# Moving four weight sums, a turn, the third unit's values and two exponentials, and cutting other products into column halves, in a fused attention and gated feed-forward kernel

## The chip, the cores and the metric

The kernel runs on one core of one Trainium2 chip. The metric is the device time of one execution in microseconds, as the median of a few runs. The core has four engines that compute: PE (TensorE, matrix products; its weight loads are listed apart as PEld), DVE (VectorE), ACT (ScalarE) and POOL (GpSimd). SP only starts DMA transfers here. The engines work through their own queues in order and meet at semaphores.

## What is computed

Sliding-window causal attention (batch 8, 8 heads, 576 positions, head size 64, window 64) is followed by a gated feed-forward layer on the 4608 resulting tokens (512 features, 1536 hidden):

```python
scores = scale * np.matmul(q, k.transpose(0, 1, 3, 2))
rel = pos[:, None] - pos[None, :]
mask = (rel >= 0) & (rel < 64)
scores = np.where(mask, scores, -1000000000.0)
attn = np.exp(scores - scores.max(-1)) ; attn = attn / (attn.sum(-1) + 1e-09)
x = np.matmul(attn, v)            # to (4608, 512)
gate = np.maximum(x @ w_gate, 0.0)
val = x @ w_val
out = (gate * val) @ w_out
```

## The kernel before

**Tiles.** The 4608 tokens are cut into tiles t=0 to t=9 of 384, 192, 448 and then 512 columns (`widths`). Attention works in windows of 64 positions; the first tokens come from units u of 192 positions (u=0, 1, 2), the rest from quads qd of four windows, two quads to a tile. For each tile the order is: scores (`q_st`, L277: 128 tiny instructions, a weight load and a matmul for each of 64 blocks), exponentials on ACT (`q_exp`, L450), masks on DVE (`q_mask`, L459), values (`t_pv`, L493: 64 weight loads and 64 matmuls of 65 columns for each half of the heads), reciprocals and scaling on DVE (L507, L515), a turn into the layout of the next product (L521), and sums of blocks of x (`x_form`, L537). Units do the same with `u_st`, `u_exp`, `u_mask`, `u_pv` (L348), `u_recip` and so on, called through `plan_exps` and `plan_values`.

**Feed-forward.** Tiles 0 and 1 use plain products: `first_hidden` and `hidden` (L634) multiply blocks of w_gate and w_val with x, ACT applies the relu (L605) and DVE multiplies the two (the gate, L609, L613, L614), and `output` (`out_mm`, L1135) multiplies by w_out. A product in `SPLIT` runs as two column halves; `halves` says how many blocks of one weight start as a group whose first two steps of four run for all, before the last two, so that the second half of the weight may land later. `OUT_SPLIT` says from which f on `out_mm` cuts its 512 columns in two, up to the last but one. From t=2 on, `fast_hidden` forms the two hidden products of each pair of blocks by seven products, P1 to P7, in place of eight (L740), which needs sums of weight blocks (`w_form`, L561, into `us` for w_gate and `vs` for w_val) and of x blocks. For a block j, the product P1 is copied by ACT to a second bank (a seed, L749), P6 and P7 are added in the first bank and copied out in between (snaps, L759); DVE adds (L776), ACT applies relu (L782, L809), DVE or POOL multiply (L765). From t=4 on, the output product is also formed with seven products (`SevenOut`, L956). `HALVED` names the products of `fast_hidden` that run as two column halves: each of its four matmuls becomes two with 128 columns, each with its own weight load.

**Order.** All is written out by hand through `Weaver`: `W.at(T, fn)` puts work into a heap at a planned time, `W.clock` is advanced by the planned length of PE's products, and `W.advance` issues what is due. The planned times only set the order in which instructions are put into the engines' queues; what an engine waits for at run time is settled by semaphores. `one_bank`, `two_banks` and `bank` hand out the eight PSUM banks; `W.pop` issues planned work until a bank is free.

**What the change touches.** `scores` (exponentials of a quad at planned times), the constants `SPLIT`, `OUT_SPLIT` and `HALVED`, the plan of the third unit's values (`plan_values(27.0, 2)`), the plan of turning q and k of batch 2 (`plan_batch(2, ...)`, executed at L200 on DVE), the list of weight sums by time, and the call of `hidden(0, ...)` with its groups. POOL copies v's rows for the third unit (`v_spread`, L216), and issues most loads (L160 weights, L162 w_out, L180 q and k, L206 v).

Of the kernel before, what the change touches and what calls it, by code (L numbers as in the profile page):

```python
# [47 lines left out]
def kernel(  # L48
# [10 lines left out]
    nc = tc.nc  # L59
# [8 lines left out]
    NF = DF // 128  # L68
    G = 4
    scale = 1.0 / float(D) ** 0.5  # L70
    TT = 2 * U
# [70 lines left out]
    W = Weaver()  # L142
# [33 lines left out]
    def qk_load(b, name, hh):  # L176

        tile_ = nat[b, name, hh] = nats[:, 2 * "kq".index(name) + hh]
        src = (q if name == "q" else k)[b, G * hh:G * hh + G]
        nc.gpsimd.dma_start(tile_, src.rearrange("h (i j) d -> (h i) (j d)", i=32))  # L180
# [241 lines left out]
    def read(to, give):  # L422
        unread.discard(id(to))
        if give:
            free.append(to)
# [4 lines left out]
    def q_wins(qd):  # L430
        return range(NQ // 64 - QW if qd == 1 else QW)

    def q_st(qd, banks=None):

        d = quads[qd] = {"st": banks or [bank() for _ in range(G)], "p": [None] * G}
        unread.update(map(id, d["st"]))
        run_rows([[st_block(d["st"][g][:, 256 * hh + 64 * i:256 * hh + 64 * i + 64], g, hh, q_window(qd, i), False, hh + i > 0)
                   for hh in range(2) for i in q_wins(qd)] for g in range(G)])
        written.update((id(to), 512) for to in d["st"])
        return 0.72  # L440

    def q_part(qd, p):
        return p.rearrange("p (h i) c -> p h i c", h=2)[:, :, 0:len(q_wins(qd))]

    def q_exp(qd, g, give=True):
        d = quads[qd]
        d["p"][g] = a_p.tile([128, 2 * QW, 64], FP16, name="pw", tag="p")
        n = 64 * len(q_wins(qd))
        if n == 256:
            nc.scalar.activation(d["p"][g].rearrange("p n c -> p (n c)"), d["st"][g], ACT.Exp, scale=scale)  # L450
        else:
            nc.scalar.activation(q_part(qd, d["p"][g]), d["st"][g].rearrange("p (h n) -> p h n", h=2)[:, :, 0:n]
                                 .rearrange("p h (i c) -> p h i c", c=64), ACT.Exp, scale=scale)
        read(d["st"][g], give)
# [10 lines left out]
    def scores(qd, T, banks=None, give=True):  # L465

        W.clock += q_st(qd, banks)
        for g in range(G):
            late = 0.8 if qd > 8 and qd % 2 and g == G - 1 else 0.0
            W.at(T + 0.8 + 0.6 * g + late, lambda g=g: q_exp(qd, g, give))  # L470
            W.at(T + 1.5 + 0.6 * g + late, lambda g=g: q_mask(qd, g))

    def t_pv(t, hh, banks, give):
# [89 lines left out]
    def plan_batch(b, load, trans):  # L563
        for i, (name, hh) in enumerate((n, hh) for n in "kq" for hh in range(2)):
            if load is not None:
                W.at(load if isinstance(load, float) else load[i], lambda name=name, hh=hh: qk_load(b, name, hh))
            if trans is None:
                continue
            W.at(trans[i], lambda name=name, hh=hh: qk_trans(b, name, hh))
# [7 lines left out]
    def plan_values(T, u):  # L577
        W.at(T, lambda: u_pv(u))
        W.at(T + 0.6, lambda: u_recip(u))
        for hh in range(2):  # L580
            W.at(T + 0.8 + 0.5 * hh, lambda hh=hh: u_norm(u, hh))
        W.at(T + 1.8, lambda: u_turn(u))
# [7 lines left out]
    def hidden(t, spans, f0=0, f1=NF, each=1, halves={}, split=(), banks=None):  # L590

        if t == 1:
            gs[2] = g_sb_p.tile([128, NF, WT], FP16, name="g_sb"), {}
        g_sb, done = gs[0]
        xt = xt_tile(t)
        n = spans[0][1] - spans[0][0]

        w = 512 // n
        each = max(each, w)

        def part(tile):
            return tile[:, 0:w * n].rearrange("p (w n) -> p w n", w=w)

        def relu(r_sb, h1):
            nc.scalar.activation(part(r_sb), part(h1), ACT.Relu)  # L605

        def gate(f, c0, r_sb, h2):
            if t == 0:
                nc.vector.tensor_tensor(g_sb[:, f:f + w, c0:c0 + n], part(r_sb), part(h2), MUL)  # L609
                done.update(dict.fromkeys(range(f, f + w), c0 + n))  # L610
                return
            m = WT - TT
            nc.vector.tensor_tensor(g_sb[:, f:f + w, TT:WT], part(r_sb)[:, :, 0:m], part(h2)[:, :, 0:m], MUL)  # L613
            nc.vector.tensor_tensor(gs[2][0][:, f:f + w, 0:n - m], part(r_sb)[:, :, m:n], part(h2)[:, :, m:n], MUL)  # L614
            done.update(dict.fromkeys(range(f, f + w), WT))
            gs[2][1].update(dict.fromkeys(((b, -1) for b in range(f, f + w)), True))

        for fb in range(f0, f1, each):
            r2s = [f_sb.tile([128, 2, WT], FP32, name="pr", bufs=4) for _ in range(2)]
            r_sbs = {}  # L620
            for i, wt in enumerate((wg, wv)):
                items = [(c0, f) for c0, _ in spans for f in range(fb, fb + each, w)]
                first = halves.get((fb, i), 1)
                for group in [items[:first]] + [[item] for item in items[first:]]:
                    hs = [singles[banks.pop(0)] if banks else one_bank() for _ in group]
                    part_written(hs)
                    for cs in ((0, 1), (2, 3)) if len(group) > 1 else (range(NC),):
                        for (c0, f), h in zip(group, hs):
                            for b in range(w):
                                W.advance(W.clock)  # L630
                                w_need(wt, f + b, cs[-1] // 2)
                                m = n // 2 if (i, f) in split else n
                                for c, lo in ((c, lo) for c in cs for lo in range(0, n, m)):
                                    nc.tensor.matmul(h[:, b * n + lo:b * n + lo + m], wt[:, c, (f + b) * 128:(f + b) * 128 + 128],  # L634
                                                     xt[:, c, c0 + lo:c0 + lo + m], start=(c == 0 and lo == 0 and not (len(group) > 1 and b)),
                                                     stop=(c == NC - 1), skip_group_check=len(group) > 1 or m < n)
                                W.clock += len(cs) * (n + 7) / 2400.0
                            if cs[-1] < NC - 1:
                                continue
                            if i == 0:  # L640
                                r_sb = r_sbs[c0, f] = r2s[len(r_sbs) // 2][:, len(r_sbs) % 2]
                                W.at(W.clock, lambda r_sb=r_sb, h=h: relu(r_sb, h))
                            else:
                                W.at(W.clock, lambda f=f, c0=c0, r_sb=r_sbs[c0, f], h=h: gate(f, c0, r_sb, h))
# [55 lines left out]
    def fast_hidden(t, seven=None):  # L700
# [23 lines left out]
        def product(j, name, i):  # L724
# [10 lines left out]
            w, x = operands(name, *kinds[i], j)  # L735
            step = HT // 2 if (t, j, name) in HALVED else HT
            for m in range(2):
# [434 lines left out]

    LAST = len(widths) - 1
    BY_ACT = ()
    SPLIT, OUT_SPLIT = [(0, 4 + i) for i in range(8)] + [(1, 4 + i) for i in range(4)], 3
    HALVED = ((4, 0, 'P5'),)
    FAST_OUT = (LAST - 5, LAST - 4, LAST - 3, LAST - 2, LAST - 1, LAST)
    O_FORMS = {3: [(1.4, 2, 0), (1.5, 2, 1), (1.6, 2, 2), (1.7, 0, 0), (1.8, 0, 1), (6.5, 0, 2), (9.0, 1, 0), (14.2, 1, 1), (14.3, 1, 2)],
               4: [(4.3 + 0.1 * j, 3, j) for j in range(3)]}
# [8 lines left out]
    with tc.manual_schedule():  # L1188
# [63 lines left out]
        w_load(*V3[2], 29.6)  # L1252
        W.at(22.0, lambda: u_st(2))
        plan_exps(22.0, 2)
        plan_values(27.0, 2)

        v_spread(2, pool)
        for name in "kq":
# [18 lines left out]
        W.at(36.4, lambda: v_spread(3, pool))  # L1277
        for u in (4, 5):
            W.at(41.9, lambda u=u: v_spread(u, dve))
        plan_batch(2, (36.5, 36.6, 38.0, 38.1), (52.9, 53.0, 57.5, 62.0))  # L1280
        W.at(50.5, lambda: behind_x(2))
        for u in (6, 7):
            W.at(38.2, lambda u=u: v_load(u))
# [46 lines left out]
                    qk_loads(t + 3, ends - QAT)  # L1330

        sums = {w: [(w, j, n) for j in range(NF // 4) for n in (0, 1, 3, 2)] for w in (0, 1)}
        for T, gap, eng, some in ((16.2, 0.0, nc.vector, sums[0][:4]), (20.9, 0.0, nc.vector, sums[1][:4] + sums[0][4:8]),
                                  (29.7, 0.0, nc.vector, sums[1][4:6]),
                                  (44.7, 0.1, nc.gpsimd, sums[1][6:8] + sums[0][8:10]), (50.6, 0.1, nc.gpsimd, sums[0][10:12] + sums[1][8:])):
            for i, (w, j, n) in enumerate(some):
                W.at(T + gap * i, lambda eng=eng, w=w, j=j, n=n: w_form(eng, (wg, wv)[w], n, j))
# [10 lines left out]

        W.advance(15.3)
        first_hidden()  # L1350
        hidden(0, ((0, TT),), 4, NF, 4, split=SPLIT, halves={(8, 0): 3, (8, 1): 2})
        hidden(1, ((0, U),), each=4, banks=[0, 1, 4, 5, 2, 3, 0, 1, 2, 3, 0, 1])
        taken["one"] += 2
        output(0, (0, 1, 2, 3), (0, 4, 8, NF))
# [4 lines left out]
        for t in range(2, LAST + 1):  # L1359
# [30 lines left out]
            qd = 2 * (t + 1 - NS)  # L1390
# [39 lines left out]
```

## Time and profile before

| | us |
|---|---|
| median of 3 runs (lowest to highest) | 301.84 (301.57 to 301.95) |
| the profiled execution: its own time | 301.29 |
| its span, first to last instruction | 299.6 |
| PE busy in the span | 288.8 |
| DVE busy | 256.7 |
| ACT busy | 198.7 |
| POOL busy | 193.9 |

Where the time goes by stage, with PE's busy time in it (from the view of stretches of time):

| stretch | what runs | length | PE busy |
|---|---|---|---|
| 20.0 to 38.5 | hidden products of t=0 and t=1, third unit | 18.5 | 18.08 |
| 38.5 to 53.8 | first scores of t=2, output of t=0 and t=1 | 15.3 | 15.18 |
| 53.8 to 116.3 | t=2 and t=3 | 62.5 | 62.44 |
| 116.3 to 147.8 | t=4 | 31.5 | 30.90 |
| 147.8 to 178.1 | t=5 | 30.3 | 30.30 |
| 178.1 to 209.2 | t=6 | 31.1 | 30.52 |
| 209.2 to 239.5 | t=7 | 30.3 | 30.30 |
| 239.5 to 299.6 | t=8, t=9 and the end | 60.1 | 56.55 |

How to read the lines that follow. A line of the timeline has the start, the time from the first start to the last end of the merged instructions, the engine, the line of the kernel, the operation, output and inputs, the tile shape and, with an x, how many; in brackets the idle time of that engine just before and what ended it. Matmuls are pipelined: one lasts some 0.2 us longer than its distance to the next, so lengths of runs are taken from start to start. A line of the view of stretches has the stretch, its length, and for each engine the busy time and the number of instructions begun. "Issue" is time in which an engine waited for nothing that the profile shows.

### The profile page before, as it was taken

The page shows a single profiled execution, that of the slowest core. Times are in us where ns is not written, and L with a number is a line of the kernel's source. Part 1 is how long each engine was busy: PE and PEld are TensorE (multiplying, and loading weights), DVE is VectorE, ACT ScalarE, POOL GpSimd, SP SyncE. Part 2 cuts the span into 40 slices and gives each one's busy share as a digit, 9 for nine tenths or more (in the row PEclk, how much of TensorE's full clock was granted, in tenths as well). Part 3 has the DMA queues.
Part 4 walks back from the last instruction along what each step waited for, and adds up shares of the span by engine and source line. Part 5 has one row for each costly group of instructions (what it writes and reads, how often), then busy time and mean ns, then how long its engine had stood idle before and what let it go on. Part 6 is the DMA issues. An engine that isn't in the chain of part 4 may idle for free.

```text
span 299.6 us, 10994 instructions
## 1 busy us (share of the span) xinstructions
PE 288.8 (96%) x4627; PEld 242.2 (81%) x4627; DVE 256.7 (86%) x513; ACT 198.7 (66%) x400; POOL 193.9 (65%) x223
## 2 busy tenths in 40 slices
PE   4899999999999999999999999999999999999995
PEld 2488878996588756888888888878888888888894
DVE  5989987797889799899999999989858986896585
ACT  3744361888378848974898479846985698637850
POOL 8767668897369926785948595859276607441751
PEclk9999999999999999999999999999999999999999
DMA  7999999966946489901599239924910210021013
GB/s 216 181 197 195 193 194 200 221 68 120 161 128 113 82 150 173 116 18 39 80 210 105 66 61 216 116 64 55 179 30 19 83 47 0 3 83 61 1 38 105
DMA packets 59122, 32.86 MB, mean 110 GB/s; under 512 B 39488, under 2 KB 53440, under 8 KB 59072
## 3 DMA queue, kind: packets, MB, share of 16 engines
q0 software_dynamic: 46688, 18.29, 52.5%
q1 hardware_dynamic: 11808, 13.41, 15.1%
q8 instruction: 36, 0.59, 0.8%
q10 hardware_dynamic: 576, 0.46, 0.5%
q14 instruction: 14, 0.11, 0.1%
HBM read 37.75 MB, written 9.44 MB: 158 GB/s over the span
## 4 chain that ended last, share of the span: by engine, by line
PE 89%; DVE 6%; DMA 1%; issue 1%; ACT 1%; DVEq 0%
PE bank L740 48%; PE bank L956 19%; PE bank L874 5%; PE bank L634 4%; PE bank L1135 4%; PE bank L493 3%; PE bank L277 3%; DVE kT L200 2%; PE bank L672 1%; DMA vs<-in_k_dram 1%; DVE qT L200 1%; DVE pw L459 1%; PE bank L348 1%; DVE p L318 1%; ACT pw L450 1%
## 5 line engine op out<-in xcount | busy, mean ns | idle before, releaser
L765 POOL TENSOR_TENSOR g_sb<-pr 128x512 f16<-128x512 f32 (+1 forms) x36 | 45.2, 1256 | 41.8 <-ACT pr L782 41.5
L776 DVE TENSOR_TENSOR pr<-bank,pr 128x512 f32<-128x512 f32 (+1 forms) x96 | 60.9, 674 | 3.3 <-PE bank L740 1.9
L759 ACT COPY pr<-bank 128x512 f32<-128x512 f32 (+1 forms) x96 | 51.0, 587 | 14.0 <-PE bank L740 13.9
L765 DVE TENSOR_TENSOR g_sb<-r,bank 128x512 f16<-128x512 f32 (+1 forms) x48 | 32.5, 677 | 22.7 <-ACT r L809 21.0
L956 PEld LDWEIGHTS <-g_sb 128*128 128x128 f16 x444 | 41.8, 98 | 5.1
L740 PE MATMUL bank<-xc,vs 128*128 128x256 f16 (+2 forms) x292 | 42.7, 269 | 0.3 <-ACT pw L450 0.3
L740 PE MATMUL bank<-xc,us 128*128 128x256 f16 (+2 forms) x292 | 42.7, 269 | 0.0
L740 PEld LDWEIGHTS <-vs 128*128 128x128 f16 x388 | 37.6, 98 | 4.3 <-issue 0.5
L740 PEld LDWEIGHTS <-us 128*128 128x128 f16 x388 | 37.6, 98 | 3.8
L206 POOL DMA_DIRECT2D v<-in_v_dram x41 | 34.7, 866 | 9.1 <-PE bank L740 3.2
L782 ACT ACTIVATE pr<-pr 128x512 f32<-128x512 f32 (+1 forms) x48 | 30.2, 630 | 8.4 <-DVE pr L776 8.4
L450 ACT ACTIVATE pw<-bank 128x512 f16<-128x512 f32 x60 | 32.1, 606 | 2.1 <-PE bank L277 1.7
L809 ACT ACTIVATE r<-bank 128x512 f32<-128x512 f32 (+1 forms) x48 | 28.7, 598 | 5.4 <-PE bank L740 4.7
L740 PEld LDWEIGHTS <-wg 128*128 128x128 f16 x288 | 28.0, 98 | 3.2
L740 PEld LDWEIGHTS <-wv 128*128 128x128 f16 x288 | 28.1, 98 | 2.9
L740 PE MATMUL bank<-xt,wg 128*128 128x256 f16 (+1 forms) x192 | 28.5, 271 | 0.0
L740 PE MATMUL bank<-xt,wv 128*128 128x256 f16 (+1 forms) x192 | 28.5, 271 | 0.0
L906 POOL TENSOR_TENSOR g_sb<-g_sb,xus 128x512 f16<-128x512 f16 x24 | 27.0, 1144 | 0.0
L956 PE MATMUL bank<-wo,g_sb 128*128 128x256 f16 (+1 forms) x222 | 26.6, 270 | 0.0
L749 ACT COPY bank<-bank 128x512 f32<-128x512 f32 (+1 forms) x48 | 25.6, 573 | 0.0
L956 PE MATMUL bank<-wts,g_sb 128*128 128x256 f16 (+1 forms) x222 | 25.6, 270 | 0.0
L459 DVE TENSOR_TENSOR pw<-pw,mask 128x512 f16<-128x512 f16 x60 | 23.5, 437 | 2.1 <-ACT pw L450 1.7
(125 smaller groups left out, 521.1 us busy)
## 6 DMA issues: line engine op xcount, KB each, us to landing
out_dram<-o_sb SPq DMA_DIRECT2D x31, 256.0 KB, 3.7
nats<-in_k_dram POOLq DMA_DIRECT2D x15, 288.0 KB, 5.9
nats<-in_q_dram POOLq DMA_DIRECT2D x15, 288.0 KB, 7.0
v<-in_v_dram POOLq DMA_DIRECT2D x31, 128.0 KB, 7.7
v<-v SPq DMA_DIRECT2D x12, 132.0 KB, 2.4
v<-v SPq DMA_DIRECT2D x24, 66.0 KB, 2.0
wg<-in_moe_w_gate_dram POOLq DMA_DIRECT2D x6, 256.0 KB, 6.7
wv<-in_moe_w_val_dram POOLq DMA_DIRECT2D x6, 256.0 KB, 8.5
```

What stands on the lines that cost most here:

```text
L206: nc.gpsimd.dma_start(v16s[b % 2][lo:hi, g, :, 0:64], v[b, :, 64 * g - 64 + lo:64 * g - 64 + hi].rearrange("h p d -> p h d"))
L450: nc.scalar.activation(d["p"][g].rearrange("p n c -> p (n c)"), d["st"][g], ACT.Exp, scale=scale)
L459: nc.vector.tensor_tensor(d["p"][g], d["p"][g], mask[:, None, :].to_broadcast([128, 2 * QW, 64]), MUL)
L740: nc.tensor.matmul(to[:, HT * m + lo:HT * m + lo + step], w[:, k, 128 * m:128 * m + 128], x[:, k, lo:lo + step], start=(first and m == 0 a ...
L749: nc.scalar.copy(at[j, "B", i][:, 0:TW], at[j, "A", i][:, 0:TW])
L759: nc.scalar.copy(pr[:, i], at[j, "A", i][:, 0:TW])
L765: eng.tensor_tensor(gh[:, f:f + 2, h], pair(r), pair(v), MUL)
L776: nc.vector.tensor_tensor(pr[:, i], to[:, 0:TW], pr[:, i], ADD)
L782: nc.scalar.activation(pr[:, 0], pr[:, 0], ACT.Relu)
L809: nc.scalar.activation(r, to[:, 0:TW], ACT.Relu)
L906: eng.tensor_tensor(to, x, y, op)
L956: nc.tensor.matmul(at[key][:, QN * m * whole:QN * m * whole + n1 - n0], A[:, 128 * m:128 * m + 128], B[:, c, n0:n1] if len(B.shape) == 3 e ...
```

## The change

The exponentials of quad 7 get other planned times (the third and fourth later, the second earlier). `SPLIT` now has all eight blocks f=4 to 11 of both weights, where it had all eight of w_gate and four of w_val. `OUT_SPLIT` goes from 3 to 7. `HALVED` takes in P1, P2, P3 and P4 of block j=1 in t=4, beside P5 of j=0. The third unit's values are planned at 26.4 in place of 27.0, the last turn of q of batch 2 at 60.0 in place of 62.0. The four sums of w_gate's second block (`sums[0][4:8]`) move from 20.9 to 45.55, still on DVE. The groups of the last four blocks in `hidden(0, ...)` become 4 and 3, from 3 and 2.

```diff
         for g in range(G):
             late = 0.8 if qd > 8 and qd % 2 and g == G - 1 else 0.0
-            W.at(T + 0.8 + 0.6 * g + late, lambda g=g: q_exp(qd, g, give))
+            W.at(T + 0.8 + ((0.0, 0.3, 1.6, 1.9)[g] if qd == 7 else 0.6 * g + late), lambda g=g: q_exp(qd, g, give))
             W.at(T + 1.5 + 0.6 * g + late, lambda g=g: q_mask(qd, g))
...
-    SPLIT, OUT_SPLIT = [(0, 4 + i) for i in range(8)] + [(1, 4 + i) for i in range(4)], 3
-    HALVED = ((4, 0, 'P5'),)
+    SPLIT, OUT_SPLIT = [(i, f) for i in range(2) for f in range(4, NF)], 7
+    HALVED = [(4, 0, 'P5')] + [(4, 1, name) for name in ('P1', 'P2', 'P3', 'P4')]
...
         plan_exps(22.0, 2)
-        plan_values(27.0, 2)
+        plan_values(26.4, 2)
...
-        plan_batch(2, (36.5, 36.6, 38.0, 38.1), (52.9, 53.0, 57.5, 62.0))
+        plan_batch(2, (36.5, 36.6, 38.0, 38.1), (52.9, 53.0, 57.5, 60.0))
...
-        for T, gap, eng, some in ((16.2, 0.0, nc.vector, sums[0][:4]), (20.9, 0.0, nc.vector, sums[1][:4] + sums[0][4:8]),
+        for T, gap, eng, some in ((16.2, 0.0, nc.vector, sums[0][:4]), (20.9, 0.0, nc.vector, sums[1][:4]), (45.55, 0.0, nc.vector, sums[0][4:8]),
                                   (29.7, 0.0, nc.vector, sums[1][4:6]),
...
-        hidden(0, ((0, TT),), 4, NF, 4, split=SPLIT, halves={(8, 0): 3, (8, 1): 2})
+        hidden(0, ((0, TT),), 4, NF, 4, split=SPLIT, halves={(8, 0): 4, (8, 1): 3})
```

In the built programs PE has 9311 instructions in its list where it had 9247, 64 more; DVE, ACT, POOL and SP have as many as before. On PE the third unit's values (L348) now stand ahead of the last group of w_gate. On DVE the four sums stand ahead of the reciprocals of t=2's first values, and the turn of q one gate and one sum earlier. On ACT one exponential of quad 7 stands ahead of a seed copy (L749). POOL's and SP's orders are the same.

## The prediction

> **What bounds the kernel now.** I read the page first (busy shares, queues, chain), then the list of PE's waits, then PE's timeline around each wait, then the instruction counts at those moments.
>
> ```profile
> PE 288.8 (96%) x4627; PEld 242.2 (81%) x4627; DVE 256.7 (86%) x513; ACT 198.7 (66%) x400; POOL 193.9 (65%) x223
> ...
> q8 instruction: 36, 0.59, 0.8%
> ```
>
> PE sets the end: it is busy for 96% of the span and has 89% of the chain that ended last. The granted clock is 9 tenths or more in every slice, so time can only come out of PE's idle stretches. The queue "instruction" is the program itself being read: 36 packets in 0.59 MB, 16 KB each. PE runs 4627 weight loads and 4627 matmuls: 9254 / 36 = 257, so a packet holds about 256 PE instructions.
>
> ```profile
> PE bank L956 <- issue: 0.6, 1, 0.6
> PE bank L634 <- DVE g_sb L609: 0.4, 1, 0.4
> PE bank L740 <- ACT pw L450: 0.3, 1, 0.3
> PE bank L493 <- issue: 0.3, 1, 0.3
> ```
>
> These are all of PE's waits of 0.3 us and more after the first 15.2 us. Two are on engines, two on "issue", which is nothing the profile names. The list counts idle time after the modelled end of a matmul, so I take the lost time from starts.
>
> ```profile
> 137.90 1.32 PE L493 MATMUL bank<-v,pw 128*32 128x65 f16 x127
> 139.48 0.19 PE L493 MATMUL bank<-v,pw 128*32 128x65 f16 x1 [0.26 <-issue]
> 139.60 1.48 PE L956 MATMUL bank<-wts,xus 128*128 128x256 f16 x12
> ...
> 168.66 1.34 PE L493 MATMUL bank<-v,pw 128*32 128x65 f16 x128
> 169.93 1.48 PE L956 MATMUL bank<-wts,xus 128*128 128x256 f16 x12
> ...
> 200.27 0.94 PE L956 MATMUL bank<-wts,xus 128*128 128x256 f16 x7
> 201.78 0.71 PE L956 MATMUL bank<-wts,xus 128*128 128x256 f16 x5 [0.58 <-issue]
> ```
>
> The same 128 value products (t_pv for both halves) take 137.90 to 139.60 = 1.70 us in t=4 and 168.66 to 169.93 = 1.27 us in t=5: 0.43 lost. In t=6 the stop comes seven matmuls later; the chain has 200.34 to 204.67 = 4.33 us for 32 matmuls where t=5 has 170.00 to 173.60 = 3.60: 0.73 lost. In t=7 the same piece is 231.31 to 234.99 = 3.68: 0.08 lost.
>
> ```profile
> 0.00:139.20 139.20, 132.78 (x2270) 104.74 (x2271) 121.52 (x241) 88.42 (x190) 100.62 (x126) 1.00 0.97 147
> 0.00:201.50 201.50, 194.53 (x3294) 159.00 (x3295) 180.37 (x355) 133.64 (x276) 144.50 (x174) 1.00 0.90 137
> 0.00:232.40 232.40, 225.15 (x3806) 185.96 (x3807) 205.09 (x404) 156.25 (x319) 164.24 (x194) 1.00 0.85 128
> ```
>
> This is the key view: PE matmuls and weight loads begun before each stop (first two counts). Sums: 4541 = 17 x 256 + 189, 6589 = 25 x 256 + 189, 7613 = 29 x 256 + 189. All three stops stand on one boundary modulo 256, so PE has run out of fetched program. The instruction packets fit: narrow windows of the DMA view put one at 136.9 and one at 199.2, each some 1.4 us long, and PE resumes 2.6 us after each begins (139.48, 201.78); the next begin 1.16 us after PE resumes (140.6, 202.9). (A packet's length is its busy share in such a window, times 16 engines.) So a block is usable about 3.7 us after PE enters the one ahead of it (1.16 + 2.6; less by what is read ahead). A burst of 256 value instructions eats a whole block in 1.1 us. It stalls where a boundary lies at the start of that burst: 4285, 6333 and 7357 are PE's counts within 25 instructions of the bursts' starts (4286 at 137.85).
>
> **The change, part by part.** Instruction counts and order are those of the two built programs.
>
> *1. Four products in halves (HALVED), and what it does to every later boundary.* P1 to P4 of j=1, t=4, for both weights: 32 matmuls of 256 columns become 64 of 128. The already halved P5 has eight from 118.15 to 118.60, 56 ns each; L740's 152 in 16.59 us are 109 each. 64 x 0.0557 - 32 x 0.109 = +0.08 us. But PE's later instructions all stand 64 further on (L493 of t=4 moves from 4279 to 4343 in the order). The boundaries fall 32 matmuls, or 32 x 0.109 = 3.5 us, earlier before each burst, and the next one inside the burst, some 192 to 216 instructions in, about 0.9 us after its start. Time from entering to needing: 3.5 + 0.9 = 4.4 us and read-ahead on top, against 3.7: the three stops go, -0.43 - 0.73 - 0.08 = -1.24 us. Next late candidate: the block entered inside the burst. In t=4 it must last through the rest of the burst (0.28), 32 matmuls with both mode changes (3.6 + 0.1) and 128 score instructions (0.6): 4.6 us against 3.7. It holds by 0.9; in t=5 to 7 by 0.5 to 1.3 more, as the boundary drifts 8 instructions a tile. t=8 splits its values in two bursts 28 matmuls apart; none fills a block. Bounds: 0 (all stops reappear elsewhere) to -1.24.
>
> A page of the Trainium skill speaks against halving: "TensorE: Matmul & The Clock Gate", Back-to-back issue gap, gives some 81 ns for each 128-column matmul in a stream with its weight loads. By it the 64 would cost 64 x 0.081 - 32 x 0.109 = +1.7 us and the sum would be near 302; this trace has 56 ns for exactly such pairs and disagrees.
>
> *2. More of w_val's in halves (SPLIT), fewer of w_out's (OUT_SPLIT).* 16 matmuls of 384 columns (29.88 to 32.48: 162.5 ns) become 32 of 192 (17.56 to 20.20: 82.5): +0.04. In the output 16 of 512 (216 ns, L874) replace 32 of 256: -0.03. The two move the boundary by +32 and back to 0 before t=2, so t=2 and t=3 see the old boundaries.
>
> *3. Four sums of w_gate moved from 20.9 to 45.55, the third unit's values from 27.0 to 26.4, groups of 4 and 3 (halves).*
>
> ```profile
> 24.41 1.85 POOL L216 COPY v<-v 64x512 f16<-64x512 f16 x2 [3.30 <-DMA v<-in_v_dram]
> 26.07 0.49 PE L634 MATMUL bank<-xt,wg 128*128 128x192 f16 x4
> 26.98 0.49 PE L634 MATMUL bank<-xt,wg 128*128 128x192 f16 x4 [0.42 <-DVE g_sb L609]
> ```
>
> DVE loses 22.47 to 24.05 = 1.58 us there, so masks and gates come early and PE's stop of 0.58 (26.98 less 26.07 less 4 x 0.0825) goes. What ends last next: the values now stand ahead of w_gate's last group and need POOL's copies, which end at 26.26: PE, ready at 26.16, starts at about 26.33. It keeps 0.4 us as far as 38.5. There the scores need DVE's gates and the turn of q:
>
> ```profile
> 36.75 1.23 DVE L200 STREAM_TRANSPOSE qT<-nats 128x576 f32<-128x576 f32 x1
> ...
> 38.16 0.27 DVE L614 TENSOR_TENSOR g_sb<-pr,bank 128x128 f16<-128x128 f32 x1
> ```
>
> DVE runs without a gap from 31.13 to 38.43, PE's scores start at 38.51: DVE is already just in time. Its run starts on w_val's f=8, which the grouping of 3 now finishes at 29.45 + 16 x 0.0825 = 30.77 against 29.88 + 6 x 0.1625 = 30.86. So of 0.4 us only 0.1 passes 38.5. A stop of about 0.28 at 52.3 (boundary 1726 = 6 x 256 + 190, its packet at 50.5 amid a full DMA) probably eats half of that: -0.05 us, bounds -0.5 (all passes) to +0.2 (that packet comes as late and DVE slips). The sums at 45.55 lie in DVE's idle 1.54 us before L507 at 47.27; 1.58 overruns by 0.05, and the t=2 products that need this chain (xc, 53.53 against P6 at 55.33) have 1.8 us of cover.
>
> *4. A turn of q from 62.0 to 60.0.* It steps ahead of one gate and one sum at 64.16 to 65.74 on DVE; the bank of that gate is next needed at 67.98, the relu behind that sum starts at 66.79 and the sum would end near 66.3. Nothing; without that cover at most its own 1.25 us.
>
> *5. Two exponentials of qd 7.* On ACT only one pair changes places: the exponential of bank 2 goes ahead of the first seed copy L749.
>
> ```profile
> 117.02 0.57 ACT L749 COPY bank<-bank 128x512 f32<-128x512 f32 x1
> ...
> 117.50 0.60 ACT L450 ACTIVATE pw<-bank 128x512 f16<-128x512 f32 x1
> ...
> 118.15 0.61 PE L740 MATMUL bank<-xc,vs 128*128 128x128 f16 x8 [0.35 <-ACT pw L450]
> ```
>
> PE is ready at 117.20 + 8 x 0.056 = 117.64 and starts at 118.15: 0.51 lost. The exponential can now start at 116.43 + 0.48 = 116.91 and end at 117.51: no wait. ACT then stays full until 119.46 (the second exponential pair ends the queue ahead of the P6 snaps), so PE's P7, due 0.5 earlier at 119.83, waits for the snap's end near 119.99, and its second half again 0.05: 0.2 is given back. -0.3, bounds -0.5 to 0.
>
> **Sum.** -1.24 + 0.08 + 0.01 - 0.05 + 0 - 0.30 = -1.50 us. The profiled execution is 301.29 (span 299.6 and 1.7 around it), so 299.8 for it; the median of the runs shown is 301.84, 0.55 above, so 300.3.
>
> **The rivals.**
> A. *The early gain passes too*: DVE's transposes slip with PE and the stop at 52.3 goes: a further -0.4 to -0.7, 299.8. For: 1.58 us do leave DVE. Against: its gapless run to 38.43.
> B. *The stops only change place*: a boundary at some other burst costs what the old cost. Then -0.05 - 0.30 + 0.09 remains, 301.6. For: t=4's margin is 0.9 us, and the packet for 1726 needed 5.6 us (47.0 to 52.7) in a full DMA. Against: DMA moves little from 135 to 142 (share 0.1).
> By the Trainium skill ("Runtime: NRT & Kernel Launch", Instruction fetch mechanics) a block is 256 instructions, which the counts above confirm, and crossing one is mostly hidden, which would also give this rival's time; the three stops at +189 disagree.
> C. *Halved products wait for their weights*: PEld's own row is 98 ns a load. If loads did not overlap, 64 x 0.098 - 32 x 0.109 = +2.8 us instead of +0.08, 303.0. It decides from 79 ns a matmul (64 x 0.023 = 1.5 us); against it stands the 56 ns of P5.
>
> **Chances.** Forecast 0.62, A 0.15, B 0.15, C and the like 0.08. About 0.2% (0.6 us) is what a measurement can tell from no change. The forecast's own range is 299.7 to 301.0; with A and B the range is 299.5 to 301.6. Faster by over 0.2% (under 301.2): forecast and A, 0.77. Within: B and a little of C, 0.16. Slower: 0.07.
>
> **What would show it.** No "issue" wait of PE at L493 and L956; the tile from 178.1 to 209.2 falls from 31.1 to the 30.3 of its neighbours; counts at any stop left again at 189 modulo 256, now elsewhere. Values of u=2 start near 26.3 and scores at 38.4. P5's second half starts right after the first, and P7 shows a small ACT wait. New L740 rows of 128 columns at 56 ns. Wrong if PE stops appear at score bursts near 143, or if PE's stops vanish and the span stays.

## The result, and the profile after

| | before | after |
|---|---|---|
| median of 6 runs each (lowest to highest) | 301.89 (301.57 to 302.45) | 299.44 (299.15 to 299.69) |
| the profiled execution: its own time | 301.29 | 299.69 |
| its span | 299.6 | 298.0 |

The ratio is 0.9916, 95% interval 0.9903 to 0.9929: the change makes the kernel 2.45 us faster by the medians. The forecast was 1.50 faster (300.3). The sign held; the size fell short by 0.95 us, below the forecast's own range (299.7 to 301.0) and just under the 299.5 of the range with rivals A and B.

From the page of the changed kernel, PE's share and the packets of program:

```profile
PE 287.5 (96%) x4659; PEld 241.8 (81%) x4659; DVE 256.0 (86%) x513; ACT 198.5 (67%) x400; POOL 194.0 (65%) x223
...
q8 instruction: 36, 0.59, 0.8%
```

PE does 32 matmuls more and is as full as before; the program is read in as many packets. All of PE's waits in the changed kernel (engine, tile and line, what it waited for, total, times, longest):

```profile
PE bank L244 <- DVE bias L130: 4.4, 1, 4.4
PE bank L277 <- DVE qT L200: 0.8, 2, 0.5
PE bank L672 <- DVE xt L391: 0.7, 1, 0.7
PE bank L672 <- DMA wv<-in_moe_w_val_dram: 0.4, 1, 0.4
PE bank L241 <- ACT p L311: 0.2, 1, 0.2
PE bank L348 <- ACT p L311: 0.2, 1, 0.2
```

The two "issue" waits at L493 and L956 are gone, and so are those of L634 on DVE and of L740 on ACT. One is new: L672 waits for a load of w_val near 17.5. From start to start that is 0.52 us lost. It is nearly this execution's alone: of the other profiles only that of e6_nohalved has it, with 0.11 (see also the second profiles below).

The chain of waits of the changed kernel around t=6's values (start, length, what):

```profile
198.27 1.27 PE bank L493 x119
199.54 3.60 PE bank L956 x32
```

The 32 output matmuls after the values take 3.60, as in the undisturbed t=5 of before, where t=6 took 4.33. In t=4 the 128 values start at 137.53 and L956 at 138.81: 1.28, where it was 1.70. Stretches of the changed kernel (stretch, length, busy time and instructions of PE, PEld, DVE, ACT and POOL, then granted clock, DMA share, GB/s):

```profile
147.00:177.30 30.30, 30.30 (x510) 26.75 (x509) 28.76 (x56) 22.58 (x45) 21.93 (x25) 1.00 0.75 114
177.30:207.60 30.30, 30.30 (x511) 26.74 (x509) 28.76 (x56) 22.58 (x44) 21.89 (x23) 1.00 0.73 113
207.60:237.90 30.30, 30.30 (x511) 26.69 (x509) 24.74 (x52) 22.66 (x45) 17.55 (x18) 1.00 0.52 79
```

Tiles 5, 6 and 7 now take 30.3 us each with PE busy throughout; t=6 took 31.1.

The early part, PE's timeline of the changed kernel around the third unit's values and its first scores of t=2 (two windows):

```profile
23.84 2.80 PE L634 MATMUL bank<-xt,wv 128*128 128x192 f16 x32
26.58 0.56 PE L348 MATMUL bank<-v,p 128*32 128x65 f16 x48
27.07 0.42 PE L634 MATMUL bank<-xt,wg 128*128 128x192 f16 x3
...
37.64 0.82 PE L634 MATMUL bank<-xt,wg 128*128 128x192 f16 x8
38.39 0.95 PE L277 MATMUL bank<-qT,kT 32*128 32x64 f16 x64
```

The values follow the products with no stop (23.84 + 32 x 0.0825 = 26.48, and the 0.1 that this change of shape takes in every profile). Inside the 64 scores lies a stop of 0.27: the first starts at 38.39 and the next at 38.67. DVE's timeline shows what is late, a gate that ends at 38.61:

```profile
36.95 1.22 DVE L200 STREAM_TRANSPOSE qT<-nats 128x576 f32<-128x576 f32 x1
38.02 0.40 DVE L613 TENSOR_TENSOR g_sb<-pr,bank 128x256 f16<-128x256 f32 x1
38.35 0.26 DVE L614 TENSOR_TENSOR g_sb<-pr,bank 128x128 f16<-128x128 f32 x1
```

At the start of t=4 (PE's timeline) P5's second half follows the first, and P7 waits a little:

```profile
117.01 0.61 PE L740 MATMUL bank<-xc,us 128*128 128x128 f16 x8
117.46 0.61 PE L740 MATMUL bank<-xc,vs 128*128 128x128 f16 x8
...
119.23 0.60 PE L740 MATMUL bank<-xt,wv 128*128 128x256 f16 x4
119.84 0.60 PE L740 MATMUL bank<-xc,us 128*128 128x256 f16 x4
120.33 0.60 PE L740 MATMUL bank<-xc,vs 128*128 128x256 f16 x4
120.77 0.61 PE L740 MATMUL bank<-xt,wg 128*128 128x128 f16 x8
121.21 0.61 PE L740 MATMUL bank<-xt,wv 128*128 128x128 f16 x8
```

119.23 to 119.84 is 0.61 where four take 0.44: 0.17 lost, and 0.05 more before 120.33. The new matmuls of 128 columns come eight in 0.445 us, 56 ns each.

### The profile page after: what moved, and what is told of

Read it like the earlier page. It is cut to its first block, busy times and chain, and to the rows that moved or that the text cites. A ratio compares the mean times of both kernels' runs of the same rounds, so it can differ in the third digit from the quotient of the medians.

```text
span 298.0 us, 11057 instructions
## 1 busy us (share of the span) xinstructions
PE 287.5 (96%) x4659; PEld 241.8 (81%) x4659; DVE 256.0 (86%) x513; ACT 198.5 (67%) x400; POOL 194.0 (65%) x223
## 4 chain that ended last, share of the span: by engine, by line
PE 90%; DMA 3%; POOL 3%; DVE 2%; issue 1%; ACT 0%; DVEq 0%; POOLq 0%
PE bank L740 49%; PE bank L956 19%; PE bank L634 6%; PE bank L874 5%; PE bank L1135 4%; PE bank L277 3%; PE bank L493 3%; DMA wv<-in_moe_w_val_dram 3%; POOL v L206 1%; PE bank L672 1%; DVE kT L200 1%; DVE pw L459 1%; POOL wg L160 0%; POOL nats L180 0%; POOL wv L160 0%
## 5 line engine op out<-in xcount | busy, mean ns | idle before, releaser
L956 PEld LDWEIGHTS <-g_sb 128*128 128x128 f16 x444 | 41.8, 98 | 5.0
L740 PE MATMUL bank<-xc,us 128*128 128x256 f16 (+2 forms) x292 | 42.7, 269 | 0.0
L740 PE MATMUL bank<-xc,vs 128*128 128x256 f16 (+2 forms) x292 | 42.7, 269 | 0.0
L740 PEld LDWEIGHTS <-vs 128*128 128x128 f16 x392 | 37.7, 98 | 3.9
L740 PEld LDWEIGHTS <-us 128*128 128x128 f16 x392 | 37.7, 98 | 3.9 <-issue 0.2
L206 POOL DMA_DIRECT2D v<-in_v_dram x41 | 34.7, 866 | 6.4 <-DMA wo<-in_moe_w_out_dram 2.5
L782 ACT ACTIVATE pr<-pr 128x512 f32<-128x512 f32 (+1 forms) x48 | 30.3, 631 | 8.4 <-DVE pr L776 8.4
L740 PEld LDWEIGHTS <-wg 128*128 128x128 f16 x300 | 28.4, 98 | 3.1
L740 PEld LDWEIGHTS <-wv 128*128 128x128 f16 x300 | 28.4, 98 | 2.7
L740 PE MATMUL bank<-xt,wg 128*128 128x256 f16 (+2 forms) x200 | 28.5, 267 | 0.0
L740 PE MATMUL bank<-xt,wv 128*128 128x256 f16 (+2 forms) x200 | 28.5, 267 | 0.0
L956 PE MATMUL bank<-wo,g_sb 128*128 128x256 f16 (+1 forms) x222 | 26.6, 270 | 0.0
L749 ACT COPY bank<-bank 128x512 f32<-128x512 f32 (+1 forms) x48 | 25.6, 577 | 0.0
L956 PE MATMUL bank<-wts,g_sb 128*128 128x256 f16 (+1 forms) x222 | 25.6, 270 | 0.0
```

The source lines that it names most:

```text
L206: nc.gpsimd.dma_start(v16s[b % 2][lo:hi, g, :, 0:64], v[b, :, 64 * g - 64 + lo:64 * g - 64 + hi].rearrange("h p d -> p h d"))
L740: nc.tensor.matmul(to[:, HT * m + lo:HT * m + lo + step], w[:, k, 128 * m:128 * m + 128], x[:, k, lo:lo + step], start=(first and m == 0 a ...
L749: nc.scalar.copy(at[j, "B", i][:, 0:TW], at[j, "A", i][:, 0:TW])
L782: nc.scalar.activation(pr[:, 0], pr[:, 0], ACT.Relu)
L956: nc.tensor.matmul(at[key][:, QN * m * whole:QN * m * whole + n1 - n0], A[:, 128 * m:128 * m + 128], B[:, c, n0:n1] if len(B.shape) == 3 e ...
```

## The experiments

Every time below is beside runs of the kernel before on the same chip; an effect in us is the ratio less one times 301.9. A "stop" is a distance between the starts of two matmuls, less what the same pair takes elsewhere.

**One part alone.** Four kernels, each the kernel before with one part of the change.

```diff
 e1_halved
-    HALVED = ((4, 0, 'P5'),)
+    HALVED = [(4, 0, 'P5')] + [(4, 1, name) for name in ('P1', 'P2', 'P3', 'P4')]
 e2_early
-        plan_values(27.0, 2)
+        plan_values(26.4, 2)
-        for T, gap, eng, some in (..., (20.9, 0.0, nc.vector, sums[1][:4] + sums[0][4:8]),
+        for T, gap, eng, some in (..., (20.9, 0.0, nc.vector, sums[1][:4]), (45.55, 0.0, nc.vector, sums[0][4:8]),
-        hidden(0, ((0, TT),), 4, NF, 4, split=SPLIT, halves={(8, 0): 3, (8, 1): 2})
+        hidden(0, ((0, TT),), 4, NF, 4, split=SPLIT, halves={(8, 0): 4, (8, 1): 3})
 e3_exps
-            W.at(T + 0.8 + 0.6 * g + late, lambda g=g: q_exp(qd, g, give))
+            W.at(T + 0.8 + ((0.0, 0.3, 1.6, 1.9)[g] if qd == 7 else 0.6 * g + late), lambda g=g: q_exp(qd, g, give))
 e4_split
-    SPLIT, OUT_SPLIT = [(0, 4 + i) for i in range(8)] + [(1, 4 + i) for i in range(4)], 3
+    SPLIT, OUT_SPLIT = [(i, f) for i in range(2) for f in range(4, NF)], 7
```

> The kernel before with only the four products of t=4 in halves. Theory 1 (the prediction's terms hold as the one profiled execution of the kernel before gives them): the stops at L493 and L956 of t=4, t=6 and t=7 go, -1.24 + 0.08 = -1.16 us, ratio 0.996; the stops at 26.3 (0.58), 52.3 (0.28) and 117.6 (0.51) stay. Theory 2 (the instruction stops vary from execution to execution and are larger on average than in the one profiled): -1.5 to -2.0 us, ratio 0.993 to 0.995, with the same profile. Rival B (stops only change place): within 0.3 us of before, with stops at other bursts.

> The kernel before with only the early part: four sums at 45.55, third unit's values at 26.4, groups of 4 and 3. Theory 1: the stop of 0.58 at 26.3 goes, some 0.25 comes back as a wait of the scores near 38.4 for DVE, so -0.3 us; and -0.6 if the stop at 52.3 goes with it. Theory 2: -0.3 us at most, the stops of t=4, 6 and 7 as before. The prediction's own term was -0.05 us.

> The kernel before with only the exponentials of quad 7 moved. Both theories: the wait of 0.51 at 117.6 goes, about 0.25 comes back as waits of P7 for the snaps of P6, so -0.26 us, ratio 0.999; the fetch stops as before.

> The kernel before with only the two lists of split products changed. By own cost +0.04 - 0.03: no change (within 0.1 us). If the fetch boundaries between 30 and 53 us, which this shifts by 32 and back, are what ends the stop at 52.3, that stop goes: -0.28 us. All other stops as before.

| kernel | median (before 301.91) | ratio, 95% interval | effect us | forecast |
|---|---|---|---|---|
| e1_halved | 300.90 | 0.9965, 0.9952 to 0.9977 | -1.06 (-1.45 to -0.69) | -1.16 |
| e2_early | 301.19 | 0.9979, 0.9966 to 0.9992 | -0.63 (-1.03 to -0.24) | -0.05 |
| e3_exps | 301.94 | 1.0007, 0.9990 to 1.0024 | +0.21 (-0.30 to +0.72) | -0.30 |
| e4_split | 301.35 | 0.9988, 0.9976 to 1.0000 | -0.36 (-0.72 to 0.00) | +0.01 |

The halved products alone end all stops in t=4, t=6 and t=7 and gain what was worked out. The early part gains more than its forecast, and the column splits of w_val and w_out, forecast at nothing, probably gain too; the profile of e4_split shows how: the stop at 52.3 is not there. The profile of e2_early has none near 26, 0.29 inside the scores and 0.18 of the stop at 52.3. The exponentials by themselves can't be told from nothing. The profile of e3_exps has their stop of 0.51 at 117.6 gone and 0.25 of new ones before P7, as forecast; the rest of that run's time is in other stops, which are larger in it (the fetch stops of t=4, t=6 and t=7 are 0.70, 0.81 and 0.32, 1.83 in sum, against 1.24 in the profile shown of before).

**Is it the count modulo 256?** The change with 12 more halved products, so that later instructions stand 256 further on than in before rather than 64, and the change without the new halved products.

```diff
 e5_256
-    HALVED = [(4, 0, 'P5')] + [(4, 1, name) for name in ('P1', 'P2', 'P3', 'P4')]
+    HALVED = [(4, 0, 'P5')] + [(4, j, name) for j in (1, 2) for name in ('P1', 'P2', 'P3', 'P4', 'P5', 'P6', 'P7')] + [(4, 0, 'P4'), (4, 0, 'P3')]
 e6_nohalved
-    HALVED = [(4, 0, 'P5')] + [(4, 1, name) for name in ('P1', 'P2', 'P3', 'P4')]
+    HALVED = ((4, 0, 'P5'),)
```

> The changed kernel with sixteen products of t=4 in halves beside the old one, in place of four, so that PE's later instructions stand 256 further on than before, one whole fetched block: the boundaries lie again where they lay. Theory 1 (the stops depend on PE's count modulo 256): the stops of t=4, t=6 and t=7 come back at 188 or 189 modulo 256, 0.6 to 1.8 us in all, and twelve more halved products cost 0.23: 300.3 to 301.4 us, ratio 0.995 to 0.998. Rival (the halves help in another way, by finer matmuls or by delaying PE): no stops, 299.7 us, ratio 0.9925.

> The changed kernel without the four halved products. Theory 1: the three stops come back at 188 or 189 modulo 256, +1.1 us on the changed kernel, 300.5 us, ratio 0.996; the stop at 52.3 stays away and so does the one at 26.3. Theory 2 (early part and halves overlap in what they win): under +0.6 us.

e5_256 ran in 301.97 (before 302.54), ratio 0.9997, 0.9974 to 1.0020; e6_nohalved in 301.06, ratio 0.9961, 0.9948 to 0.9973. The stops are back in both. In e6_nohalved they are 0.08 in t=4, 0.64 in t=6 and 0.33 in t=7, and there is one of 0.14 in t=5; against its expectation there is also a stop of 0.24 near 26. PE's timeline of e5_256 in t=4 and t=6 (two windows):

```profile
138.46 1.32 PE L493 MATMUL bank<-v,pw 128*32 128x65 f16 x127
140.01 0.19 PE L493 MATMUL bank<-v,pw 128*32 128x65 f16 x1 [0.23 <-issue]
...
200.80 0.94 PE L956 MATMUL bank<-wts,xus 128*128 128x256 f16 x7
202.31 0.71 PE L956 MATMUL bank<-wts,xus 128*128 128x256 f16 x5 [0.58 <-issue]
```

and the instructions begun up to these two stops and that of t=7, from its stretches:

```profile
0.00:139.80 139.80, 133.62 (x2398) 106.42 (x2399) 121.59 (x241) 88.14 (x190) 100.46 (x126) 1.00 0.97 146
0.00:201.80 201.80, 195.35 (x3422) 160.67 (x3423) 180.12 (x353) 133.37 (x276) 144.35 (x174) 1.00 0.90 136
0.00:233.00 233.00, 226.04 (x3934) 187.66 (x3935) 205.14 (x405) 155.97 (x319) 164.09 (x194) 1.00 0.85 128
```

Matmuls and weight loads sum to 4797, 6845 and 7869: each 256 more than in before (4541, 6589, 7613), again 189 modulo 256. So it is the place of the boundary in the burst, not the halving itself, that ends the stops. They sum to 1.20 us here (0.40, 0.74, 0.06); the 12 products cost 12 / 4 x 0.08 = 0.24, and this execution started its products about 1.2 us later than that of the changed kernel, which lost 0.52 soon after: 1.20 + 0.24 + 0.68 = 2.12, and the spans differ by 300.1 - 298.0 = 2.1. The time of e5_256 came out above what was expected (ratio 0.995 to 0.998), with an interval that reaches into it; why that execution started later is not shown. Taken out of the whole change, the halving is worth (0.9961 - 0.9916) x 301.9 = 1.4 us.

**What of the early part?** The change with the four sums back at 20.9:

```diff
-        for T, gap, eng, some in (..., (20.9, 0.0, nc.vector, sums[1][:4]), (45.55, 0.0, nc.vector, sums[0][4:8]),
+        for T, gap, eng, some in (..., (20.9, 0.0, nc.vector, sums[1][:4] + sums[0][4:8]),
```

> The changed kernel with the four weight sums back at 20.9 on DVE, all else as changed. Theory 1 (the early part wins by taking 1.6 us off DVE ahead of the masks, which POOL's copy stretches): PE stops again for masks or gates near 26, 0.9 to 1.1 us, of which some 0.25 comes off the wait at 38.4: +0.5 to +0.9 us on the changed kernel, 300.0 to 300.3, ratio 0.9935 to 0.995. Rival (the order of the values and the groups alone does it): as the changed kernel, 299.4.

It ran in 300.05, ratio 0.9923, 0.9911 to 0.9936. The time is one that theory 1 named, but by the ratio it can't be told from the change (0.9916). PE's stops near 26 sum to 0.33, not 0.9 to 1.1, and the wait of 0.27 inside the scores is still there. So the sums matter less than I took them to: standing the values ahead of w_gate's last group fills most of the stop by itself, since PE has 48 value matmuls to do while DVE's gates come.

**The exponential pair later.** The change with the fourth exponential of quad 7 put 0.5 later, behind the snaps that P7 waits for:

```diff
-            W.at(T + 0.8 + ((0.0, 0.3, 1.6, 1.9)[g] if qd == 7 else 0.6 * g + late), lambda g=g: q_exp(qd, g, give))
+            W.at(T + 0.8 + ((0.0, 0.3, 1.6, 2.4)[g] if qd == 7 else 0.6 * g + late), lambda g=g: q_exp(qd, g, give))
```

> The changed kernel with the last exponential of quad 7 planned at 2.4 in place of 1.9, which puts it behind the first P6 snap on ACT. Theory: the wait of P7 for that snap (0.18 in t=4) goes, the second half's wait of 0.05 stays: -0.15 us, not to be told from no change by the median, but seen in the trace. If ACT's queue were not what holds P7, the wait stays.

It ran in 299.46, ratio 0.9912, 0.9898 to 0.9927: no better than the change. P7's first wait of 0.18 is gone, and the one before its second half grows from 0.05 to 0.23. ACT is full there (busy from 117.0 to 120.5 without a gap); the order only chooses which half waits.

**Both kernels profiled once more**, unedited, one run each.

> The kernel before once more, for a second profile of it. Theory (the one profiled execution of before had an unusually short early stop): the masks of the third unit take 0.7 us and more while POOL copies v, PE's stops between 25.5 and 27 sum to 0.9 to 1.1 us (profile shown before: 0.58) and the third unit's scores start after 38.8 (38.52). The rival (the profile shown is typical): 0.5 to 0.65 us and scores at 38.5. Both: the stops at 188 or 189 modulo 256 in t=4 and t=6 are there again.

> The changed kernel once more, for a second profile of it. Theory (the wait of 0.5 us for a load of w_val near 17.5 belongs to the one execution profiled): no such wait, first values of the third unit at 26.0 to 26.4, span 297.4 to 297.8. Rival (the change brings that wait, since w_val's halves now begin earlier): the wait is there again and the span stays at 298.0. Both: no stop at t=4, t=6 and t=7.

The first expectation failed. The second profile of before (its own time 300.80) has the same masks of 0.35, 0.35, 0.77 and 0.72 us, an early stop of 0.57 and scores at 38.42; its fetch stops are 0.31, 0.42 and none. The profile shown of before was not a rare one in its early part. For the changed kernel (299.77) the load of w_val is not waited for; but the execution starts its products 0.6 us later (14.41 against 13.79), a delay that is there by 9.7, so the third unit's values start at 26.68 and its span is 298.1 all the same. Neither profile of the changed kernel has a stop at t=4, t=6 or t=7. With the accidents taken out the two pairs give 299.6 - 298.0 + 0.5 = 2.1 us and 299.1 - 298.1 + 0.6 = 1.6.

What the second profile of the changed kernel adds is POOL and DVE around v's copy (two timelines, cut into windows so that each instruction has its line):

```profile
23.72 0.60 POOL L216 COPY v<-v 64x512 f16<-64x512 f16 x1 [2.85 <-DMA v<-in_v_dram]
24.38 1.05 POOL L216 COPY v<-v 64x1024 f16<-64x1024 f16 x1
...
23.92 0.62 DVE L318 TENSOR_TENSOR p<-p,mask 128x384 f16<-128x384 f16 x1 [0.85 <-ACT p L311]
24.46 1.19 DVE L318 TENSOR_TENSOR p<-p,mask 128x384 f16<-128x384 f16 x1
...
26.31 0.35 DVE L318 TENSOR_TENSOR p<-p,mask 128x384 f16<-128x384 f16 x1
```

The same mask takes 0.35 us by itself and 0.62 or 1.19 beside a copy. The copies end at 24.32 and 25.43, the masks at 24.54 and 25.65: both 0.22 later, as if a mask could only begin its work when the copy was over. In e3_exps it is 24.53 and 25.65 against 24.74 and 25.85. A gate (L609), which has one input in a PSUM bank, takes 0.54 us with a copy beside it or without.

**Is it POOL's copy?** Before, and the change, with that copy made by a DMA:

```diff
 e11_copy_dma (before), e12_after_dma (the change)
-        v_spread(2, pool)
+        v_spread(2)
```

> Before, with the copy of v's rows for the third unit made by a DMA in place of POOL; nothing else. Theory (POOL's copy stretches DVE's masks and sums): all masks of the third unit take 0.34 to 0.36 us, PE's stop near 26 falls under 0.3 us, and the time falls by 0.2 to 0.6 us if the DMA lands before the values need it (about 26.5), else the values wait for it. Rival (the masks vary by themselves or by DMA traffic): some masks still take 0.7 us or more and the stop stays at 0.6 to 1.1.

> The changed kernel with that copy made by a DMA; nothing else. Theory: masks at 0.35 us; the values of the third unit stand earlier here (26.1 to 26.6), so the DMA must land by 26.2; if it does, the time is 299.2 to 299.5 (the gain is lost at 38.4, where DVE's gates set the start of the scores), if it lands later it is 299.5 to 300.5. Rival (DVE's stretch still costs in the changed kernel): 298.8 to 299.1.

DVE's timeline of e11_copy_dma:

```profile
23.94 0.89 DVE L318 TENSOR_TENSOR p<-p,mask 128x384 f16<-128x384 f16 x3
24.75 0.55 DVE L609 TENSOR_TENSOR g_sb<-pr,bank 128x384 f16<-128x384 f32 x1
25.21 0.35 DVE L318 TENSOR_TENSOR p<-p,mask 128x384 f16<-128x384 f16 x1
```

All four masks take 0.35 us and PE has no stop near 26: the copy was the cause. As a cure it is no use. The DMA engines are full there, the copy took 5.4 and 6.9 us to land, and PE waits for it (timeline of e11_copy_dma):

```profile
25.96 0.82 PE L634 MATMUL bank<-xt,wg 128*128 128x192 f16 x8
31.22 0.75 PE L348 MATMUL bank<-v,p 128*32 128x65 f16 x48 [4.44 <-DMA v<-v]
```

306.26 against 302.05, ratio 1.0142, 1.0118 to 1.0167; with the change 307.82, ratio 1.0207, 1.0184 to 1.0229. The wait costs more than its length. After it the granted clock is 0.5 from 31.4 to 34.8 (31.3 to 34.7 in e12_after_dma), and w_gate's products of 192 columns come 160 ns apart in place of 82.5. The scores start at 43.91 against 38.52 in before, 5.4 later: the wait is 4.6 of it, 0.7 was saved ahead of it, and so some 1.5 is the clock. Both hopes of a gain failed on the landing, and e12_after_dma came out far above the 300.5 that was the most expected. Whether the changed kernel still pays for the copy can't be read from e12_after_dma. No kernel tried beats the changed one by more than its interval.

## Why the prediction was too small

| step | forecast | stops in the profiles shown, before to after | alone |
|---|---|---|---|
| 1 halved products | -1.16 | 1.24 to 0, and 0.08 for the halving: -1.16 | -1.06 |
| 2 column splits | +0.01 | the stop at 52.3, 0.28 to 0: -0.28 | -0.36 |
| 3 early part | -0.05 | near 26 and at 38.4, 0.58 to 0.27: -0.31 | -0.63 |
| 4 turn of q | 0 | 0 | not tried |
| 5 exponentials | -0.30 | 0.51 to 0.25: -0.26 | +0.21 |
| sum | -1.50 | -2.01 | -1.84 |

**Step 1 held** in count, cause and size. The boundary fell where it was worked out, no later burst stalled (rival B), and the halved matmuls took 56 ns (rival C). The Trainium skill's 81 ns for such a matmul ("TensorE: Matmul & The Clock Gate", Back-to-back issue gap) did not show. e5_256 is the proof: a further shift that brings the count back to 189 brings the stops back.

Two readings in step 1 were incomplete. The undisturbed t=5 has its boundary in the same place (5565 = 21 x 256 + 189) and no stop in before, so the count says where a stop can fall and not that it does. In the stops of all profiles PE resumed 2.2 to 2.9 us after the packet began. In before that packet began 1.2 us ahead of the values in t=5 (167.47 against 168.66), and PE reached the boundary 2.8 us after it; in t=4 it began 1.0 ahead, in t=6 0.2 behind (199.17 against 198.99). What sets the packet's start is not shown. And the margin left is narrower than the 0.9 us that was worked out with 3.7: in the changed kernel's t=4 the next packet begins at 139.69 and its block is entered at 142.90, 3.2 us later.

**Step 3 is the one that failed, by its size.** It said that "of 0.4 us only 0.1 passes 38.5" and that the stop at 52.3 "probably eats half of that". In kind it was right: the scores do wait for DVE at 38.4. But the gain was sized too small twice.

First, the prediction took 0.17 off the 0.58 for values that wait for v's copy, and 0.3 of the rest for DVE. In e2_early the values don't wait: the copies end at 25.60 and the values start at 26.04. So PE gives DVE the start of its gapless run earlier too. That run is 7.3 us long in both, and begins at 30.75 against 31.13 in before; less the 0.12 by which e2_early started its products earlier, this is 0.26 earlier, where 0.09 was worked out. What is lost at 38.4 is 0.27 in the profile shown, and 0.3 passes.

Second, the stop near 26 is often larger than in the one execution I read. It was 0.58 and 0.57 in the two profiles of before, and 0.93, 1.05 and 1.05 in e1_halved, e3_exps and e4_split, whose early part is that of before. How large depends on when v lands: where POOL's long copy starts at 25.10 or 25.20, only a mask of 0.72 waits for it; where it starts at 24.6 to 24.7, it holds a mask for 1.19 us, or in e1_halved a weight sum for 1.25. The mean of the five is 0.84; less the 0.27 that DVE then takes at 38.4, 0.57 passes, and e2_early measured 0.63.

In the changed kernel PE does the values while DVE is held. Its second profile has no stop though the long copy comes early (24.38), but its products also start late; e6_nohalved, with the same early part and the copy at 24.45, stops for 0.24 inside the values, until the fourth mask is done. So the new order takes most of the stop, not always all. The price was thus taken from one sample of a stop that varies by 0.5 us, and the copy, which I had only watched for when it ends, also slows the engine beside it.

**Step 2 hid a gain.** I took t=2's boundaries as unmoved and let the stop at 52.3 stand, inside step 3 as a loss and at nothing here. Five of the six profiles with the old splits have it (before 0.28, then 0.38, 0.14, 0.18 and 0.41), the eight with the new ones don't. The block ahead of it is not entered much earlier: in all of them that falls 0.1 to 0.2 us after the start of t=2's first values, near 47 us (52 in the two kernels with the DMA copy). But the packet began 3.3 to 3.5 us after that entry in the five, and 1.5 to 1.8 with the new splits (0.7 in e12_after_dma). The sixth with old splits is e11_copy_dma, whose tile 2 runs 5 us later: its packet began 1.1 us after the entry, in a DMA as full (share 1.25), and there is no stop. So the old splits alone don't make it. Narrow windows of the DMA view show that packet in before, begun at 50.46, and in the changed kernel, begun at 48.57:

```profile
q0 software_dynamic: 307, 0.20, 121.7%
q8 instruction: 1, 0.02, 5.4%
```

```profile
q0 software_dynamic: 109, 0.22, 106.7%
q8 instruction: 1, 0.02, 5.5%
```

Both stand in a DMA that is full (the two are the windows 50.4 to 51.5 and 48.5 to 49.6; the columns are packets, MB and share). What lets it start sooner with the new splits is not shown; no run was made for it.

**Step 5** was right in each stop. That it doesn't show in the time of e3_exps lies within that run's interval, which reaches to -0.30, the forecast.

**Rival A** (299.8: the early gain passes too and the stop at 52.3 goes) had the outcome, with the chance 0.15. Its cause was half right: DVE still holds the scores for 0.27 us, and the stop at 52.3 goes with the splits rather than with the early part (e2_early keeps 0.18 of it). Of the 2.45 us by the medians the profiles shown explain 2.01, and with the mean early stop of five profiles 2.3. The rest probably lies in executions that were not profiled: both profiled ones of before (301.29 and 300.80) are below the medians of their runs (301.89 and 302.05). Which stops are larger in the others is not known; e3_exps, whose fetch stops sum to 1.83, shows how far they can go.

## What to carry to other kernels

Look at a stop in several executions before giving it a price: those that hang on a load's landing or on a fetch varied here by half a microsecond and more, and the median is not that of the one that was profiled. Count instructions up to each unexplained stop; if the counts agree modulo a block, a few instructions more far ahead of it may be worth more than any change near it. When an engine's operations take longer in one place than in another, look for what its neighbour does in the same microsecond, and put work that doesn't depend on it in between.

## What the hardware showed that was not expected

POOL's copy of fp16 within SBUF holds DVE's two-input operations until it ends: masks of 0.35 us took 0.62 to 1.20, ending 0.20 to 0.22 us after the copy, and 0.35 when the copy was taken away. The copy can be held too: begun 0.05 us after one of DVE's sums (e4_split), it took 0.83 us in place of 0.60. The Trainium skill ("SBUF — State Buffer", Who interferes with whom) has this as an exclusive lock on a port pair that the two engines share, which a DVE operation with two inputs in SBUF needs and one with a single SBUF input doesn't, outside the modes that take both ports; the traces agree on both, with gates at 0.54 us throughout.

The 256 PE instructions of a tile's values, begun within 1.2 us, can outrun the fetch of the next block. The same stop measured 0.08 to 0.70 us in t=4, none to 0.14 in t=5, 0.35 to 0.81 in t=6 and none to 0.33 in t=7, over the kernels whose boundary stands at 189.

A wait of PE can cost more than its length: after 4.4 us without a matmul the granted clock was 0.5 for 3.4 us (e11_copy_dma and e12_after_dma).
